# Attention: transpositions issued between similarity matmuls of 384 keys each

## The chip, the cores and the metric

The kernel runs on one core of one Trainium2 chip. The metric is the device time of one execution in microseconds. The kernel before takes 780.84 us, the median of three runs (780.04 to 780.89).

## What is computed

Two batches of eight heads of attention over 768 tokens with 64 dimensions, in which a query sees only the keys of its own cluster (the nearest of 16 centroids), and two feed-forward layers behind it. All is float32.

```python
mask = q_assign[:, :, :, None] == k_assign[:, :, None, :]
scores = scale * np.matmul(q, k.transpose(0, 1, 3, 2))
scores = np.where(mask, scores, -1000000000.0)
scores = scores - np.max(scores, axis=-1, keepdims=True)
attn = np.exp(scores)
attn = attn / (np.sum(attn, axis=-1, keepdims=True) + 1e-09)
return np.matmul(attn, v).astype(np.float32)
```

Behind the attention come h = x @ w_in, a rational function of h, its product with w_out, and a gated layer (w_gate, w_val, w_out of the second layer). The change does not touch these.

## The kernel before

The attention goes through 8 pairs of heads (`pairs`). Of a pair it takes two halves of 384 queries (`half`), of a half three blocks of 128 queries (`i`), of a block the two heads (`e`). This gives 96 steps in the list `order`; n numbers them, and n modulo 12 is the place in the pair. A step n does the following.

- `scores` (L370 to L384): four similarity matmuls on PE. L376 multiplies the high and low parts of 128 queries (`q1`, the weights) by all keys (`k1`), cut by `CUT` into 512 and 256 keys, L380 adds the remaining product and the 16 rows of the mask (`q2`, `k2`, 80 rows), cut in the same way. The result is s_ps, 128 queries by 768 keys, one of two buffers of the pool `ps_s` in PSUM. There are four banks for the two.
- `maximum` (L386): DVE takes the negative maximum of each row of s_ps (L389).
- `transposes` (L425) of step n - 2 (`LAG` = 2): six transpositions of 128 by 128 of the exponentials p on PE (L435), three into one buffer t_ps, three into the next. The buffers come from the pool `ps_t` (L159), which has three; the other users of that pool in the loop are the matmuls of the clusters (`sims`, one buffer per pair) and r_ps in `spread`. Each t_ps is copied to SBUF, by ACT (L440), or the second of a step by DVE (L438) where n modulo 12 is in `dve_evac` = (2, 8, 10, 11).
- `exponentials` (L393): ACT writes p and the sums of the rows (L397).

The main loop (L601) goes over n in twos and calls these in the order scores, maximum, transposes, exponentials; where n modulo 6 is 2 and n is over 6, `spread` (L409) follows, which transposes the reciprocals of the sums (L412, r_ps) and copies them by ACT (L414). After each second step two of the six key blocks of the earlier half are multiplied by v (L446, o_ps, eight matmuls). `background` adds loads, splits and cluster steps for the next pair at fixed n.

Nothing reorders this: every engine takes its instructions in the order in which the code calls them, and waits on semaphores that follow from the tiles and buffers. PE's weight loads are rows of their own in the trace (PEld).

Of the kernel before, what the change touches and what calls it, by code (L numbers as in the profile page):

```python
# [8 lines left out]
F32 = mybir.dt.float32  # L9
F32R = mybir.dt.float32r  # L10
AF = mybir.ActivationFunctionType
ALU = mybir.AluOpType
AX = mybir.AxisListType
# [7 lines left out]
def tile_kernel(ctx, tc, q_t, k_t, q_s, k_s, v_l, cent, w_in, w_out, a_co, b_co, w_gate, w_val, w_o2, out):  # L21
    nc = tc.nc
    B, H, D, S = q_t.shape
    D //= 2
    NC = cent.shape[0] // H
    P = 128
    NB = S // P
    HALF = S // 2
    HB = NB // 2
# [9 lines left out]
    def r32(ap):  # L39
        return ap.bitcast(F32)  # L40
# [100 lines left out]
    def pool(stack, name, bufs, side, space=None):  # L141
        kw = {} if space is None else {"space": space}
        return stack.enter_context(tc.tile_pool(name=name, bufs=bufs, side=side, reuse_waits="tile", **kw))
# [16 lines left out]
    ps_s = pool(Bs, "ps_s", 2, "right", PSUM)  # L160

    heads = {}
    live = {}
    pairs = [(b, hp) for b in range(B) for hp in range(H // 2)]
    order = [(b, hp, half, i, e) for b, hp in pairs for half in range(2) for i in range(HB) for e in range(2)]
    PER = 2 * HB
    KM = D + NC
    CUT = [(0, 512), (512, S)]

    n_x = [0]  # L170

# [37 lines left out]
    def t_tile(name):  # L209
        return ps_t.tile([P, HB, P], F32, tag="t", name=name)  # L210

    def keep_warm(n, to, x=None):
        for _ in range(n):
            for j in range(HB):
                nc.tensor.transpose(to[:, j, :], ident if x is None else x[:, 0:P], ident)  # L215

    warm = ps_s.tile([P, S], F32, tag="s", name="w_ps")[:, 0:HALF].rearrange("p (j c) -> p j c", c=P)
    keep_warm(5, warm)

    wt_i = const.tile([P, NC], mybir.dt.int32, name="wt_i")  # L220
# [11 lines left out]
    for e in range(2):  # L232
# [12 lines left out]
        out=ss[:, 2:3], in0=ss[:, 0:1], scalar=ss[:, 2:3], in1=ss[:, 1:2], op0=ALU.mult, op1=ALU.add  # L245
# [121 lines left out]
                        out=r32(heads[b, 2 * hp + e][key])[D:KM, half * HALF:(half + 1) * HALF], in_=t3[g:g + NC, :]  # L367
                    )

    def scores(b, hp, half, i, e):  # L370
        t = heads[b, 2 * hp + e]
        s_ps = ps_s.tile([P, S], F32, tag="s", name="s_ps")
        q0 = half * HALF + i * P
        qs = slice(q0, q0 + P)
        for lo, hi in CUT:
            nc.tensor.matmul(s_ps[:, lo:hi], t["q1"][:, qs], t["k1"][:, lo:hi], start=True, stop=False)  # L376
        if (b, hp, half, i, e) == order[0]:
            keep_warm(6, fill, oh[0])
        for lo, hi in CUT:
            nc.tensor.matmul(s_ps[:, lo:hi], t["q2"][0:KM, qs], t["k2"][0:KM, lo:hi], start=False, stop=True)  # L380
        if (i, e) == (0, 0):
            st = live["st", b, hp, half] = st_p.tile([P, 3, PER], F32, tag="st", name="st")
            nc.vector.memset(st[:, 2, :], 1e-9)
        live["s", b, hp, half, i, e] = s_ps  # L384

    def maximum(b, hp, half, i, e):  # L386
        st = live["st", b, hp, half]
        k = e * HB + i
        nc.vector.tensor_reduce(  # L389
            out=st[:, 0, k:k + 1], in_=live["s", b, hp, half, i, e], axis=AX.X, op=ALU.max, negate=True  # L390
        )

    def exponentials(b, hp, half, i, e):  # L393
        st = live["st", b, hp, half]
        k = e * HB + i
        p = live["p", b, hp, half, i, e] = p_p.tile([P, S], F32, tag="p", name="p")
        nc.scalar.activation(  # L397
            out=p, in_=live.pop(("s", b, hp, half, i, e)), func=AF.Exp, bias=st[:, 0, k:k + 1],
            accum_out=st[:, 1, k:k + 1],
        )  # L400

    def reciprocals(b, hp, half):
        st = live["st", b, hp, half]
        nc.vector.tensor_reduce(
            out=st[:, 0, :], in_=st[:, 1:3, :].rearrange("p a k -> p k a"), axis=AX.X, op=ALU.add
        )
        nc.vector.reciprocal(out=st[:, 0, :], in_=st[:, 0, :])

    def spread(b, hp, half):  # L409
        st = live.pop(("st", b, hp, half))  # L410
        r_ps = t_tile("r_ps")[0:PER, 0, :]
        nc.tensor.transpose(r_ps, st[:, 0, :], ident)  # L412
        rs = rs_p.tile([PER, P], F32, tag="rs", name="rs")
        nc.scalar.copy(out=rs, in_=r_ps)  # L414
        rd = tc.dram_tile([2, HALF], F32, name="rd")
        nc.sync.dma_start(out=rd.rearrange("e (i p) -> (e i) p", p=P), in_=rs)
        live["rd", b, hp, half] = rd

    def bring_back(b, hp, half):
        rd = live.pop(("rd", b, hp, half))  # L420
        rb = live["rb", b, hp, half] = rb_p.tile([P, HALF], F32, tag="rb", name="rb")
        for e in range(2):
            nc.sync.dma_start(out=rb[e * D:(e + 1) * D, :], in_=rd[e:e + 1, :].to_broadcast([D, HALF]))

    def transposes(b, hp, half, i, e, on_dve):  # L425
        p = live.pop(("p", b, hp, half, i, e))
        if i == 0:
            live["pt", b, hp, half, e] = pt_p.tile([P, NB, HALF], F32, tag="pt", name="pt")
        pt = live["pt", b, hp, half, e]
        qc = slice(i * P, (i + 1) * P)  # L430
        for g in range(2):
            t_ps = t_tile("t_ps")
            for j in range(HB):
                kb = g * HB + j
                nc.tensor.transpose(t_ps[:, j, :], p[:, kb * P:(kb + 1) * P], ident)  # L435
            ks = slice(g * HB, (g + 1) * HB)
            if g == 1 and on_dve:
                nc.vector.tensor_copy(out=pt[:, ks, qc], in_=t_ps)  # L438
            else:
                nc.scalar.copy(out=pt[:, ks, qc], in_=t_ps)  # L440
# [11 lines left out]
    def normalised(b, hp, half):  # L452
        x = live["x", b, hp, half] = x_p.tile([P, HALF], F32, tag="x", name="x")
        nc.vector.tensor_tensor(
            out=x, in0=live.pop(("o", b, hp, half)), in1=live.pop(("rb", b, hp, half)), op=ALU.mult
        )
# [36 lines left out]
    def k_rest(t, x):  # L493
# [6 lines left out]
        out=h0["q1"][up, :], in0=xs[0][0:D, :], scalar=scale, in1=r32(h0["q1"][0:D, :]),  # L500
# [15 lines left out]
    cols = [slice(0, HALF), slice(HALF, S)]  # L516
# [6 lines left out]
    def q_rows(t, half):  # L523
        nc.scalar.activation(
            out=t["q2"][D:D + 32, cols[half]], in_=t["t3"][32 * half:32 * half + 32, :],
            func=AF.Identity, scale=MASKED, bias=msk[32 * half:32 * half + 32, 1:2],
        )
# [9 lines left out]
    dve_evac = (2, 8, 10, 11)  # L537
# [54 lines left out]
    LAG = 2  # L592
    def next_weighted():
        if pv:
            step = pv.pop(0)
            weighted(*step)
            if step[3] == NB - 1:
                return step[:3]


    for n0 in range(0, len(order) + LAG, 2):  # L601
        for n in (n0, n0 + 1):
            if n < len(order):
                scores(*order[n])
                maximum(*order[n])
            if n == 1:
                keep_warm(3, fill)
            if n >= LAG:
                transposes(*order[n - LAG], n % (2 * PER) in dve_evac)
            if n < len(order):  # L610
                exponentials(*order[n])
            if n == 1:
                q_rows(h1, 1)
                for t in (h0, h1):
                    del t["t3"]
            if n % PER == 0 and n:
                reciprocals(*order[n - 1][:3])
            if n % PER == RS and n > PER:
                spread(*order[n - RS - 1][:3])
            elif n == len(order) + 1:  # L620
                spread(*order[-1][:3])
            if n % PER == BB and n > PER:
                bring_back(*order[n - BB - 1][:3])
            for engine in ("dma", "pe", "dve", "pool", "act"):
                background(n, engine)
        finished = next_weighted()
        finished = next_weighted() or finished
        if finished:
            normalised(*finished)
            split_x(*finished)  # L630
        if n >= LAG and (n - LAG) % PER == PER - 1:
            pv.extend([order[n - LAG][:3] + (kb,) for kb in range(NB)])
# [13 lines left out]
    with ExitStack() as mctx:  # L646
# [15 lines left out]
            out=root[:, 1:2], in0=babs[:, 1:2], scalar=root[:, 2:3], in1=root[:, 1:2], op0=ALU.mult, op1=ALU.add  # L662
        )
        nc.vector.tensor_scalar(
            out=root[:, 0:1], in0=root[:, 1:2], scalar1=0.5, scalar2=0.0, op0=ALU.mult, op1=ALU.add
# [273 lines left out]
        for n in range(NS):  # L939
            t, f = seq[n][:2]  # L940
# [19 lines left out]
            if pipe:  # L960
                _, reciprocal, quotient, remainder = pipe.pop()
# [140 lines left out]
        LAG = {"act": 1.7, "dve": 1.7, "pool": 3.5, "dma": 5.5, "set": 0.0}  # L1102
# [105 lines left out]
        _, reciprocal, quotient, remainder = pipe.pop()  # L1208
        mm, _ = project(*seq[NS - 3])
# [12 lines left out]
        mm, _ = project(*seq[NS - 2])  # L1222
# [137 lines left out]
        j, c = 2 * u, 2  # L1360
        r0_ = j * C3 + c * P
        for a in range(2):
            ns = slice(a * 256, (a + 1) * 256)
            bank, to = ps_a.tile([P, T], F32, tag="acc", name="acc")[:, 0:256], part2(j, c)[:, a, :]
            for ff in (f - 1, f):
                g, w = g_hl[j, ff], wt_of["p", ff]
                for m, (wi, gi) in enumerate(((0, 0), (1, 0), (0, 1))):
                    nc.tensor.matmul(  # L1368
                        bank, g[:, gi, c * P:(c + 1) * P], w[:, wi, ns], start=(ff < f and m == 0),
                        stop=(ff == f and m == 2),  # L1370
# [51 lines left out]
```

## Time and profile before

| | |
|---|---|
| median of 3 runs | 780.84 us |
| span of the profiled execution, from its first to its last instruction | 779.4 us |
| PE busy | 773.3 us (99%) |
| weight loads (PEld) busy | 637.7 us (82%) |
| DVE busy | 594.4 us (76%) |
| ACT busy | 510.9 us (66%) |
| POOL busy | 457.4 us (59%) |
| transpositions L435, 576 | 78.7 us |
| similarity matmuls L376, 192 | 58.4 us in the page's group, 512 keys: 490 ns mean, 256 keys: 281 ns |

The granted TensorE clock is 1.00 over the span. Matmuls are pipelined: a row's duration reaches from the start of a matmul to its end, and the next one starts before that, so durations do not add up to the time on the path. What a matmul costs PE is read from the distance of the starts. The attention stage ends with the last transpositions at 227 us.

### The profile page before, as it was taken

Reading aid. Unit: us, or ns where it says so; the run is one execution under the profiler, and the core shown is the slowest. Engines: PE = TensorE matmul, PEld = TensorE weight load, DVE = VectorE, ACT = ScalarE, POOL = GpSimd, SP = SyncE. Lnnn points to the kernel's source line nnn. Section 1 sums busy time; section 2 is a strip of 40 time slices with the busy share of each in tenths; the row PEclk is TensorE's granted clock in tenths of the full one; section 3 lists DMA queues with packets and bytes.
Section 4 is the critical chain, followed back from the end, with each engine's and each line's share of the span. In section 5 each row is a group of like instructions: output and inputs, shape, how many; then the busy total and the mean of one; then the engine's idle time right before and its main releaser. Section 6 shows DMA issues by size and latency. Waiting matters only on the chain.

```text
span 779.4 us, 11585 instructions
## 1 busy us (share of the span) xinstructions
PE 773.3 (99%) x4119; PEld 637.7 (82%) x4119; DVE 594.4 (76%) x894; ACT 510.9 (66%) x984; POOL 457.4 (59%) x429
## 2 busy tenths in 40 slices
PE   8999999999999999999999999999999999999998
PEld 7666666666767888888888888999999999999997
DVE  7778787778659999989999999997565655675454
ACT  8777777777776788787777768646645545454331
POOL 6476797678334676767777688764354544534410
PEclk9999999999999999999999999999999999999999
DMA  7266436533322211211211111013222112120013
GB/s 224 76 203 205 153 99 202 178 115 114 98 79 78 81 56 66 70 55 56 81 55 53 56 33 49 27 55 100 90 82 81 55 55 82 55 81 28 1 41 122
DMA packets 27209, 67.94 MB, mean 87 GB/s; under 512 B 4464, under 2 KB 10832, under 8 KB 27152
## 3 DMA queue, kind: packets, MB, share of 16 engines
q1 hardware_dynamic: 27152, 67.21, 26.3%
q8 instruction: 32, 0.52, 0.3%
q14 instruction: 25, 0.20, 0.1%
HBM read 59.48 MB, written 3.19 MB: 80 GB/s over the span
## 4 chain that ended last, share of the span: by engine, by line
PE 98%; DVE 1%; SPq 1%; DMA 0%; ACT 0%; issue 0%; POOL 0%; POOLq 0%
PE c_ps L1012 23%; PE h_ps L695 17%; PE acc L751 17%; PE acc L1069 13%; PE o_ps L446 8%; PE t_ps L435 8%; PE s_ps L376 5%; PE s_ps L380 4%; PE w_ps L215 1%; PE sim L305 1%; SPq L366 1%; DMA k<-t 0%; DVE st L389 0%; PE r_ps L412 0%; PE acc L1368 0%
## 5 line engine op out<-in xcount | busy, mean ns | idle before, releaser
L1012 PE MATMUL c_ps<-r,wb 128*128 128x384 f32 x648 | 125.3, 336 | 0.0
L1012 PEld LDWEIGHTS c_ps<-r,wb 128*128 128x128 f32 x648 | 115.4, 188 | 6.0
L389 DVE TENSOR_REDUCE st<-s_ps 128x1 f32<-128x768 f32 x96 | 91.5, 953 | 31.3 <-PE s_ps L380 30.5
L397 ACT ACTIVATE p<-s_ps,st 128x768 f32<-128x768 f32 x96 | 87.7, 913 | 13.6 <-DVE st L389 13.3
L712 POOL TENSOR_TENSOR tmp<-tmp 128x512 f32<-128x512 f32 x46 | 67.9, 1475 | 48.1 <-ACT tmp L711 47.7
L440 ACT COPY pt<-t_ps 128x384 f32<-128x384 f32 x160 | 70.0, 482 | 37.8 <-PE t_ps L435 37.5
L1020 ACT COPY tmp<-c_ps 128x384 f32<-128x384 f32 x60 | 28.8, 480 | 87.3 <-PE c_ps L1012 87.3
L1091 POOL TENSOR_TENSOR part<-tmp,part 128x512 f32<-128x512 f32 x18 | 23.3, 1297 | 101.0 <-ACT tmp L1090 101.0
L435 PE MATMUL t_ps<-ident,p 128*128 128x128 f32 x576 | 78.7, 272 | 0.0
L446 PE MATMUL o_ps<-pt,v 128*64 128x384 f32 x384 | 72.3, 499 | 0.0
L435 PEld LDWEIGHTS t_ps<-ident,p 128*128 128x128 f32 x576 | 66.8, 141 | 4.7 <-issue 0.6
L735 POOL TENSOR_TENSOR g<-td,tmp 128x512 fp32r<-128x512 f32 x45 | 58.5, 1300 | 18.0 <-DVE td L730 18.0
L751 PE MATMUL acc<-g,r 128*128 128x512 f32 x288 | 69.0, 389 | 0.0
L1023 DVE TENSOR_TENSOR tmp<-tmp,c_ps 128x384 f32<-128x384 f32 x40 | 22.2, 555 | 58.9 <-ACT tmp L1020 45.1
L1012 PE MATMUL c_ps<-r,xw 128*128 128x384 f32 x336 | 65.4, 337 | 0.0
L751 PEld LDWEIGHTS acc<-g,r 128*128 128x128 f32 x288 | 54.0, 188 | 11.2
L1012 PEld LDWEIGHTS c_ps<-r,xw 128*128 128x128 f32 x336 | 60.0, 188 | 3.7
L695 PE MATMUL h_ps<-r 128*128 128x512 f32 x252 | 60.8, 391 | 0.0
L1069 PE MATMUL acc<-wb,g 128*128 128x512 f32 x216 | 59.4, 394 | 0.0
L376 PE MATMUL s_ps<-k,q 128*128 128x512 f32 x192 | 58.4, 385 | 0.2 <-ACT p L397 0.2
L695 PEld LDWEIGHTS h_ps<-r 128*128 128x128 f32 x252 | 47.1, 188 | 11.5 <-issue 1.8
L376 PEld LDWEIGHTS s_ps<-k,q 128*128 128x128 f32 x192 | 28.8, 189 | 31.7 <-ACT pt L440 18.0
(169 smaller groups left out, 1774.3 us busy)
## 6 DMA issues: line engine op xcount, KB each, us to landing
raw<-w_in_dram SPq DMA_DIRECT2D x16, 512.0 KB
raw<-w_out_dram SPq DMA_DIRECT2D x16, 512.0 KB
raw<-w_val_dram SPq DMA_DIRECT2D x12, 512.0 KB
raw<-w_gate_dram SPq DMA_DIRECT2D x12, 512.0 KB
raw<-w_o_dram SPq DMA_DIRECT2D x12, 512.0 KB
xa<-q_t_dram SPq DMA_DIRECT2D x14, 384.0 KB
xa<-k_t_dram SPq DMA_DIRECT2D x14, 384.0 KB
sq<-q_s_dram SPq DMA_DIRECT2D x8, 384.0 KB
```

The lines of the kernel that those rows point to most:

```text
L376: nc.tensor.matmul(s_ps[:, lo:hi], t["q1"][:, qs], t["k1"][:, lo:hi], start=True, stop=False)
L389: nc.vector.tensor_reduce(out=st[:, 0, k:k + 1], in_=live["s", b, hp, half, i, e], axis=AX.X, op=ALU.max, negate=True)
L397: nc.scalar.activation(out=p, in_=live.pop(("s", b, hp, half, i, e)), func=AF.Exp, bias=st[:, 0, k:k + 1], accum_out=st[:, 1, k:k + 1],)
L435: nc.tensor.transpose(t_ps[:, j, :], p[:, kb * P:(kb + 1) * P], ident)
L440: nc.scalar.copy(out=pt[:, ks, qc], in_=t_ps)
L446: nc.tensor.matmul(live["o", b, hp, half][e * D:(e + 1) * D, :], heads[b, 2 * hp + e]["v"][:, kb, :], live["pt", b, hp, half, e][:, kb, :] ...
L695: nc.tensor.matmul(h_ps, w[:, wi, cs], x[:, xi, cc, :], start=(n == 0), stop=(n == 3 * NCC - 1))
L712: spread.tensor_tensor(out=tq, in0=tq, in1=tr, op=ALU.add)
L735: eng.tensor_tensor(out=g[:, 1, :], in0=td, in1=tr, op=ALU.mult)
L751: nc.tensor.matmul(acc[c], w[:, wi, cs], g[:, gi, :], start=(first and m == 0), stop=(last and m == 2))
L1012: nc.tensor.matmul(live2[key], set_of[f][:, wi, a, cs], x[xi][:, kc, :], start=(first and n == 0), stop=(n == last), skip_group_check=True,)
L1069: nc.tensor.matmul(acc2[j, c], g[:, gi, c * P:(c + 1) * P], w[:, wi, :], start=(f % 2 == 0 and m == 0), stop=(f % 2 == 1 and m == 2),)
```

## The change

Each similarity matmul now takes 384 keys: the first two go to the first and the second bank of s_ps, which is now two banks of 512 with 384 columns used in each, the last two add to them. `transposes` has become a generator that stops after every transposition but the last. The loop makes it before `scores`, and `scores` takes one transposition from it behind each similarity matmul; what is left, two transpositions and the second copy, comes after `maximum`. The maximum and the exponentials read s_ps as two pieces of 384. The keys' halves `cols` were there before (0 to 384, 384 to 768).

```diff
-    def scores(b, hp, half, i, e):
+    def scores(b, hp, half, i, e, behind):
         t = heads[b, 2 * hp + e]
-        s_ps = ps_s.tile([P, S], F32, tag="s", name="s_ps")
+        s_ps = ps_s.tile([P, 2, 512], F32, tag="s", name="s_ps")[:, :, 0:HALF]
         q0 = half * HALF + i * P
         qs = slice(q0, q0 + P)
-        for lo, hi in CUT:
-            nc.tensor.matmul(s_ps[:, lo:hi], t["q1"][:, qs], t["k1"][:, lo:hi], start=True, stop=False)
+        for n in range(2):
+            nc.tensor.matmul(s_ps[:, n], t["q1"][:, qs], t["k1"][:, cols[n]], start=True, stop=False)
+            behind()
         if (b, hp, half, i, e) == order[0]:
             keep_warm(6, fill, oh[0])
-        for lo, hi in CUT:
-            nc.tensor.matmul(s_ps[:, lo:hi], t["q2"][0:KM, qs], t["k2"][0:KM, lo:hi], start=False, stop=True)
+        for n in range(2):
+            nc.tensor.matmul(
+                s_ps[:, n], t["q2"][0:KM, qs], t["k2"][0:KM, cols[n]], start=False, stop=True
+            )
+            behind()
...
-            out=st[:, 0, k:k + 1], in_=live["s", b, hp, half, i, e], axis=AX.X, op=ALU.max, negate=True
+            out=st[:, 0, k:k + 1], in_=live["s", b, hp, half, i, e], axis=AX.XY, op=ALU.max, negate=True
...
                 nc.tensor.transpose(t_ps[:, j, :], p[:, kb * P:(kb + 1) * P], ident)
+                if (g, j) != (1, HB - 1):
+                    yield
...
         for n in (n0, n0 + 1):
+            turns = transposes(*order[n - LAG], n % (2 * PER) in dve_evac) if n >= LAG else iter(())
             if n < len(order):
-                scores(*order[n])
+                scores(*order[n], lambda: next(turns, None))
                 maximum(*order[n])
             if n == 1:
                 keep_warm(3, fill)
-            if n >= LAG:
-                transposes(*order[n - LAG], n % (2 * PER) in dve_evac)
+            for _ in turns:
+                pass
```

On PE, before: the transposition of r_ps at the end of step n = 8, and step n = 9 up to the first matmuls with v (o_ps). The number behind a name tells buffers and tiles apart; in brackets stands the engine whose semaphore is waited for.

```order
L412 MATMUL r_ps_499<-ident_130,st_298 6x128 [waits DVE_49,Activation_49]
L376 MATMUL s_ps_509<-k1_189,q1_187 128x512 [waits Activation_49]
L376 MATMUL s_ps_509<-k1_189,q1_187 128x256
L380 MATMUL s_ps_509<-k2_190,q2_188 128x512
L380 MATMUL s_ps_509<-k2_190,q2_188 128x256
L435 MATMUL t_ps_516<-ident_130,p_474 128x128 [waits Activation_49]
L435 MATMUL t_ps_516<-ident_130,p_474 128x128 x2
L435 MATMUL t_ps_521<-ident_130,p_474 128x128 [waits DVE_49]
L435 MATMUL t_ps_521<-ident_130,p_474 128x128 x2
```

The same place on PE in the changed kernel:

```order
L415 MATMUL r_ps_499<-ident_130,st_298 6x128 [waits DVE_49,Activation_49]
L375 MATMUL s_ps_509<-k1_189,q1_187 128x384 [waits Activation_49]
L438 MATMUL t_ps_512<-ident_130,p_474 128x128 [waits Activation_49]
L375 MATMUL s_ps_509<-k1_189,q1_187 128x384
L438 MATMUL t_ps_512<-ident_130,p_474 128x128
L380 MATMUL s_ps_509<-k2_190,q2_188 128x384
L438 MATMUL t_ps_512<-ident_130,p_474 128x128
L380 MATMUL s_ps_509<-k2_190,q2_188 128x384
L438 MATMUL t_ps_520<-ident_130,p_474 128x128 [waits DVE_49]
L438 MATMUL t_ps_520<-ident_130,p_474 128x128 x2
```

Four of the six transpositions have moved between and behind the similarity matmuls; the last similarity matmul now has three transpositions ahead of it. The wait for ACT ahead of the first transposition and the wait for DVE ahead of the fourth were there before.

On DVE, before, around the same place: the maximum of n = 8 (s_ps_480), the copy of that step's second transpositions, and on to the maximum of n = 9 (s_ps_509).

```order
L389 TENSOR_REDUCE st_439<-s_ps_480 128x1 [waits PE_49]
L438 COPY pt_486<-t_ps_492 128x3x128 [waits PE_49]
L348 TENSOR_TENSOR sm_429<-wt_153,mx_402 128x384 [waits DVE_49]
L354 TENSOR_SCALAR sm_429<-sm_429,msk_156 128x384 [waits DVE_49]
L389 TENSOR_REDUCE st_439<-s_ps_509 128x1 [waits PE_49]
```

On DVE in the changed kernel:

```order
L392 TENSOR_REDUCE st_446<-s_ps_480 128x1 [waits PE_49]
L443 COPY pt_482<-t_ps_491 128x3x128 [waits PE_49]
L347 TENSOR_TENSOR sm_429<-wt_153,mx_402 128x384 [waits DVE_49]
L353 TENSOR_SCALAR sm_429<-sm_429,msk_156 128x384 [waits DVE_49]
L392 TENSOR_REDUCE st_446<-s_ps_509 128x1 [waits PE_49]
```

Nothing has moved on DVE: the copy still stands behind the maximum of its step.

## Rows read from the trace of the kernel before

**Rows 1.** The page: busy time, share, instructions; chain that ended last, by engine.

```profile
PE 773.3 (99%) x4119; PEld 637.7 (82%) x4119; DVE 594.4 (76%) x894; ACT 510.9 (66%) x984; POOL 457.4 (59%) x429
...
PE 98%; DVE 1%; SPq 1%; DMA 0%; ACT 0%; issue 0%; POOL 0%; POOLq 0%
```

**Rows 2.** Waits of PE: tile, line <- what ended it: us in total, times, longest.

```profile
PE w_ps L215 <- POOL ident masks.py:199: 1.4, 1, 1.4
PE s_ps L380 <- DMA k<-t: 0.7, 1, 0.7
...
PE s_ps L376 <- ACT p L397: 0.2, 1, 0.2
```

**Rows 3.** Timeline of PEld, step n = 88: start, us from first to last, instruction, count.

```profile
208.20 0.30 PEld L376 LDWEIGHTS s_ps<-k,q 128*128 128x128 f32 x2 [0.60 <-ACT pt L440]
208.54 0.31 PEld L380 LDWEIGHTS s_ps<-k,q 80*128 80x128 f32 x2
208.89 0.70 PEld L435 LDWEIGHTS t_ps<-ident,p 128*128 128x128 f32 x6
209.56 0.30 PEld L376 LDWEIGHTS s_ps<-k,q 128*128 128x128 f32 x2
```

**Rows 4.** Timeline of PE at 600 us: matmuls of 384 and of 512 columns.

```profile
600.27 1.03 PE L1012 MATMUL c_ps<-r,xw 128*128 128x384 f32 x5
601.14 0.86 PE L1069 MATMUL acc<-xw,g 128*128 128x512 f32 x3
601.84 0.85 PE L1069 MATMUL acc<-tdw,g 128*128 128x512 f32 x3
```

**Rows 5.** Groups of PE by line and shape: count | busy us, mean ns | idle before.

```profile
L1012 PE MATMUL c_ps<-r,wb 128*128 128x384 f32 x648 | 125.3, 336 | 0.0
...
L380 PE MATMUL s_ps<-k,q 80*128 80x256 f32 x96 | 27.1, 282 | 0.0
...
L412 PE MATMUL r_ps<-ident,st 128*6 128x128 f32 x16 | 4.4, 273 | 0.0
```

**Rows 6.** Timeline, steps n = 86 and 87; in brackets idle time before, and what ended it.

```profile
204.73 0.96 DVE L389 TENSOR_REDUCE st<-s_ps 128x1 f32<-128x768 f32 x1 [0.34 <-PE s_ps L380]
...
205.19 0.30 PEld L376 LDWEIGHTS s_ps<-k,q 128*128 128x128 f32 x2
...
205.61 0.55 DVE L438 COPY pt<-t_ps 128x384 f32<-128x384 f32 x1
...
206.23 0.14 PEld L435 LDWEIGHTS t_ps<-ident,p 128*128 128x128 f32 x1
```

**Rows 7.** Timeline: accumulator of n = 27, first load of n = 29.

```profile
73.21 0.19 ACT L397 ACTIVATION_READ_ACCUMULATOR p<-s_ps,st 128x1 f32 x1
...
73.73 0.30 PEld L376 LDWEIGHTS s_ps<-k,q 128*128 128x128 f32 x2
```

**Rows 8.** Timeline: maximum and exponentials of n = 6, first load of n = 8.

```profile
23.04 0.94 DVE L389 TENSOR_REDUCE st<-s_ps 128x1 f32<-128x768 f32 x1
...
24.15 0.97 ACT L397 ACTIVATE p<-s_ps,st 128x768 f32<-128x768 f32 x1
...
24.95 0.26 ACT L397 ACTIVATION_READ_ACCUMULATOR p<-s_ps,st 128x1 f32 x1
...
25.26 0.30 PEld L376 LDWEIGHTS s_ps<-k,q 128*128 128x128 f32 x2 [0.26 <-ACT p L397]
```

**Rows 9.** Timeline: accumulator of n = 95, first load of its transpositions.

```profile
226.18 0.19 ACT L397 ACTIVATION_READ_ACCUMULATOR p<-s_ps,st 128x1 f32 x1
...
226.43 0.14 PEld L435 LDWEIGHTS t_ps<-ident,p 128*128 128x128 f32 x1
```

**Rows 10.** The page's costliest groups: two copies by ACT, three-dimensional and flat.

```profile
L440 ACT COPY pt<-t_ps 128x384 f32<-128x384 f32 x160 | 70.0, 482 | 37.8 <-PE t_ps L435 37.5
L1020 ACT COPY tmp<-c_ps 128x384 f32<-128x384 f32 x60 | 28.8, 480 | 87.3 <-PE c_ps L1012 87.3
```

More of the change, by code (lines that the diff above doesn't have):

```diff
@@ L167, in tile_kernel @@
     KM = D + NC
-    CUT = [(0, 512), (512, S)]
     n_x = [0]
@@ L215, in keep_warm @@
                 nc.tensor.transpose(to[:, j, :], ident if x is None else x[:, 0:P], ident)
-    warm = ps_s.tile([P, S], F32, tag="s", name="w_ps")[:, 0:HALF].rearrange("p (j c) -> p j c", c=P)
+    warm = ps_s.tile([P, 2, 512], F32, tag="s", name="w_ps")[:, 0, 0:HALF].rearrange("p (j c) -> p j c", c=P)
     keep_warm(5, warm)
@@ L397, in exponentials @@
         nc.scalar.activation(
-            out=p, in_=live.pop(("s", b, hp, half, i, e)), func=AF.Exp, bias=st[:, 0, k:k + 1],
-            accum_out=st[:, 1, k:k + 1],
+            out=p.rearrange("p (a n) -> p a n", a=2), in_=live.pop(("s", b, hp, half, i, e)), func=AF.Exp,
+            bias=st[:, 0, k:k + 1], accum_out=st[:, 1, k:k + 1],
         )
```

## The prediction

> **What bounds the kernel now.** I read the page's first and fourth parts, then the list of waits, then the timeline of the stretch that the change touches. PE is busy for 773.3 of 779.4 us and is 98% of the chain that ended last [rows 1]. The list of PE's waits has five lines; the longest is 1.4 us, at the start, the next 0.7 us, the shortest 0.2 us [rows 2]. So nothing late on another engine costs time today, and whatever lengthens PE's own queue moves the end one for one. The attention stage fills PE from about 9.5 to 225.7 us with 96 steps; I call them by n, 0 to 95. 94 of them (n = 2 to 95) hold four similarity matmuls and the six transpositions of step n-2.
>
> **What a step costs on PE.** The weight loads give its rhythm, since one starts when the matmul before it starts. In the step at 208.20 the first load of the similarities' first pair starts at 208.20, that of the second pair at 208.54, that of the first transposition at 208.89, that of the next step at 209.56 [rows 3]: 0.34 + 0.35 + 0.67 = 1.36 us. The six transpositions take 0.67 us, 0.11 each: each has 128 columns and waits for its own load, which starts only with the transposition before. After the last one the next similarity's load also takes 0.11, so 0.34 - 0.11 = 0.23 us are left for the matmul of 512 keys, and 0.35 - 0.23 = 0.12 for that of 256. The loads of both lie under columns.
>
> **The change, part by part.**
>
> *Slots on PE.* Loads and matmuls stay as many; their order becomes similarity, transposition, four times, and two more transpositions. Under 384 columns the transposition's load is hidden; but the load of the similarity behind it now starts with the transposition, and shows its 0.11 us as it does today behind the sixth. Uncovered loads: today five of transpositions and one of a similarity, afterwards two and four. So the six slots of 0.11 us stay, and what differs is 2 x (0.23 + 0.12) = 0.70 us against four matmuls of 384. Rows of that width stand late in the kernel: five in 601.14 - 600.27 = 0.87 us, 0.174 each; three of 512 there take 601.84 - 601.14 = 0.70, 0.233 each [rows 4], about the 0.23 here. The lower bound is 4 x 0.173 = 0.69 us (-0.01 a step), the upper 4 x 0.184 = 0.736 (+0.035), if a change of operand at every slot costs 0.01. I take 0.178, 0.712 us: +0.012 x 94 = **+1.1 us**, bounds -0.9 and +3.3. So I expect nothing from the interleaving itself.
>
> *The maximum comes later.* VectorE's maximum needs the last similarity matmul, now in the seventh slot. It started 0.11 + 0.23 + 0.12 + 0.23 = 0.69 us into the step; now 0.11 + 3 x (0.178 + 0.11) = 0.97. A matmul of 384 columns also takes 336 ns from start to end against 282 for 256 [rows 5]. Together **0.34 us later**. VectorE was idle before the maximum of 204.73, which PE released [rows 6], so it shifts in full.
>
> *Who waits for that: the fourth transposition of fifteen steps.* The transpositions' results go round three buffers (ps_t, L159); a step takes two, one for each three keys' blocks. When `spread` (L409) adds r_ps as a third, the second half of the next step gets the buffer of the second half of the step before, whose copy in those steps runs on VectorE, behind the maximum: the order shows the wait on DVE. Today, in n = 86: maximum at 204.73, copy 205.61 to 206.16, load of the fourth transposition at 206.23 [rows 6], 0.07 us to spare. Afterwards the copy ends at 206.16 + 0.34 = 206.50. The next step's first load starts at about 205.20 (205.19 today [rows 6]), its last similarity 0.97 later at 206.17, and the fourth transposition's load could start then and its matmul at 206.17 + 0.178 = 206.35. The load waits: 206.50 + 0.05 for the release (25.21 to 25.26 [rows 8]) = 206.55, its matmul 206.66: **0.31 us of idle PE**, nothing hides it, and the two transpositions and o_ps queue behind. Were only the matmul held, it would be 206.55 - 206.35 = 0.20; 0.40 if the copy slips another 0.09 (VectorE has other work). r_ps comes 16 times [rows 5], the last behind the last similarity: 15 x 0.30 = **+4.5 us**, bounds 3.0 and 6.0. Below zero it cannot go while the shift exceeds 0.07.
>
> *Who else waits.* A step's first similarity needs the exponentials of two steps before. The tightest place in the steady state is n = 27, whose accumulator is read until 73.21 + 0.19 = 73.40 with the load at 73.73 [rows 7]: 0.33 against a shift of 0.34. Since n = 27 is itself one of the fifteen, its successors come 0.30 later, and I cost it at **nothing**; without that cover it is 0.01 to 0.1 us at a few odd steps. At the start no o_ps fills PE, and n = 8 waits for the exponentials today: maximum 23.04 to 23.98, exponentials from 24.15, (of n = 6) read until 25.21, load at 25.26 [rows 8]. Shifted, the maximum ends at 24.32 and the exponentials start at about 24.42, +0.27. Two such rounds in a row: **+0.5 us** (0.2 to 0.7). At the end the exponentials of n = 95 end at 226.37 and the load of their transposition follows at 226.43 [rows 9]: **+0.3 us**. In n = 13 PE waits 0.71 us for a DMA in front of the third similarity [rows 2]; now two transpositions stand before it: **-0.2 us**. Copies, exponentials and maxima read three-dimensional patterns; that is 482 ns against 480 for a flat copy of the same size [rows 10], so nothing. ScalarE's, GpSimd's and SyncE's queues keep their order.
>
> **Sum.** 1.1 + 4.5 + 0.5 + 0.3 - 0.2 = +6.2 us. The profiled execution's span is 779.4 us; the median of the runs, 780.84, has 1.4 more around it, which stay. 780.84 + 6.2 = **787.0 us**.
>
> **The rivals.**
>
> *Loads vanish on both sides (faster).* If a similarity's load were taken up before the transposition ahead of it starts, both would be covered, and the four slots in front of similarities would shrink to their columns. From the two widths, (0.23 - 0.12) / 256 x 128 = 0.055, plus 0.01 that is left of 0.12 at 256 columns: 0.065 instead of 0.11. 4 x 0.045 x 94 = -17 us: 787.0 - 17 = 770. It decides from the point at which a second load may wait behind a running matmul. Against it: the loads' rows start one matmul apart throughout; six transpositions in a row never fall below 0.11 [rows 3]. Chance 0.08. The Trainium skill bears on this (TensorE: Matmul & The Clock Gate, Step-by-step: what each phase is for): PE's queue pulls weight loads ahead of running matmuls, into a background buffer. By that rule alone the change ought to win, but here the trace shows one load ahead and not two. The same page (Back-to-back issue gap) has 81 ns for a sustained pair with 128 columns; by that the gain would be an estimated 4 x 0.029 x 94 = 11 us; the trace's 0.11 us disagrees.
>
> *The wait has no teeth.* If the copy still ends before the fourth load (the maximum shifts less, or the scheduler's release is another), the sum is 1.1 + 0.5 + 0.3 - 0.2 = 1.7: 782.5, with the slots' bounds 780.5 to 784.7. For it: only 0.3 us decides, and 0.07 are spare. Against: every term of the shift has a row. Chance 0.18, of which 0.08 lands within 0.2%.
>
> *Maximum, exponentials and the next similarity become the bound (slower still).* If the banks apart make the two reads slower by 0.1 us each, the shift is 0.54, the fifteen waits grow by 0.2 (+3), and the first similarities at two odd steps of each of the eight pairs of heads, with 0.33 to 0.48 to spare, wait about 0.07 (+1): 791. For it: the shift alone uses up the spare time of [rows 7]; against, [rows 10]. Chance 0.14.
>
> **How the numbers follow.** The forecast, 784.7 to 789.5, has 0.58, the rivals 0.08, 0.18 and 0.14, and 0.02 are left for no change by other ways. The range of 781.5 to 791.5 takes in all of the forecast, most of the second rival and the third, and leaves out the first. A measurement of this kernel can tell about 0.2%, 1.6 us, from no change: faster 0.08, same 0.10, slower 0.82.
>
> **What would show it.** In the profile after: the load row of the next step 1.36 to 1.40 us behind in steps without o_ps; similarity and transposition in pairs of 0.29 us; fifteen idle gaps of some 0.3 us on PE before the fourth transposition of odd steps, released by the copy on DVE; maxima starting 1.35 us into a step and not 1.01; the attention stage ending some 6 us later and everything behind it unchanged. Pairs of 0.25 us or less would prove the slots wrong; no gaps, the wait.

## The result, and the profile after

The changed kernel takes **786.3 us** (median of 4 runs, 786.22 to 786.87) against 780.5 of the kernel before beside it (780.04 to 780.89): a ratio of **1.0074 [1.0059, 1.0088]**, 0.7% slower. The profiled spans are 785.1 and 779.4 us. The prediction was 787.0, in a range of 781.5 to 791.5, with 0.82 on slower.

The page of the changed kernel, busy time by engine and the chain that ended last, answers to [rows 1].

```profile
PE 778.5 (99%) x4119; PEld 641.2 (82%) x4119; DVE 592.6 (75%) x894; ACT 516.5 (66%) x984; POOL 457.7 (58%) x429
...
PE 97%; DVE 1%; POOL 1%; ACT 1%; issue 0%; POOLq 0%; ACTq 0%
```

PE still bounds the kernel, with as many instructions. Its busy time has grown by 5.2 us, and part of that is no work: the row of a similarity is 0.42 us long, while the next matmul starts 0.26 us behind it where nothing holds it (227.16 and 227.42 us), and so the row covers part of a wait that follows. That is why the largest new row stands among the waits of the weight loads and not among those of PE. Waits of the weight loads (tile and line, what ended the wait, us in total, times, longest), kernel after:

```profile
PEld t_ps L438 <- DVE pt L443: 4.0, 14, 0.3
...
PEld s_ps L375 <- ACT p L400: 1.9, 4, 0.7
```

The first of the two rows is new; the second was 1.1 us in four waits before. In the waits of PE, the same columns, ScalarE's exponentials now hold up a similarity three times and not once as in [rows 2]:

```profile
PE s_ps L375 <- ACT p L400: 0.9, 3, 0.4
```

To see where the 5.7 us lie I cut both traces at the same places: the first similarity matmul of n = 0, 14 and 94, and the o_ps that follow the last transpositions (more o_ps come later, between the matmuls of the next layer). PE timeline (start, us from first to last, instruction, count) of before:

```profile
9.53 0.60 PE L376 MATMUL s_ps<-k,q 128*128 128x512 f32 x2
...
40.54 0.62 PE L376 MATMUL s_ps<-k,q 128*128 128x512 f32 x2
...
221.39 0.62 PE L376 MATMUL s_ps<-k,q 128*128 128x512 f32 x2
...
227.46 1.51 PE L446 MATMUL o_ps<-pt,v 128*64 128x384 f32 x8
```

and of after (the window of this view ends within the last row's group):

```profile
9.88 0.60 PE L375 MATMUL s_ps<-k,q 128*128 128x384 f32 x2
...
41.33 0.45 PE L375 MATMUL s_ps<-k,q 128*128 128x384 f32 x1
...
226.85 0.44 PE L375 MATMUL s_ps<-k,q 128*128 128x384 f32 x1
...
233.18 1.19 PE L451 MATMUL o_ps<-pt,v 128*64 128x384 f32 x6
```

| stretch | before | after | difference |
|---|---|---|---|
| up to n = 0 | 9.53 | 9.88 | +0.35 |
| n = 0 to 14 | 31.01 | 31.45 | +0.44 |
| n = 14 to 94 | 180.85 | 185.52 | +4.67 |
| n = 94 to those o_ps | 6.07 | 6.33 | +0.26 |
| behind, to the end of the span | 551.9 | 551.9 | 0 |

The first line is no effect of the change, which has done nothing by then: over all profiles of this study n = 0 starts between 9.1 and 10.1 us. The second line hides more than it shows, since before holds a wait for a DMA in it that after does not have (below). Everything behind the attention stage is as long as it was.

### The profile page after: what moved, and what is told of

The parts are those of the page before. It is cut to its first block, busy times and chain, and to the rows that moved or that the text cites. A ratio compares the mean times of both kernels' runs of the same rounds, so it can differ in the third digit from the quotient of the medians.

```text
span 785.1 us, 11637 instructions
## 1 busy us (share of the span) xinstructions
PE 778.5 (99%) x4119; PEld 641.2 (82%) x4119; DVE 592.6 (75%) x894; ACT 516.5 (66%) x984; POOL 457.7 (58%) x429
## 4 chain that ended last, share of the span: by engine, by line
PE 97%; DVE 1%; POOL 1%; ACT 1%; issue 0%; POOLq 0%; ACTq 0%
PE c_ps L1018 23%; PE h_ps L701 17%; PE acc L757 17%; PE acc L1075 13%; PE o_ps L451 9%; PE t_ps L438 8%; PE s_ps L375 5%; PE s_ps L380 4%; PE sim L304 1%; DVE st L392 1%; PE w_ps L214 1%; ACT p L400 1%; POOL k L499 0%; POOL q L502 0%; PE r_ps L415 0%
## 5 line engine op out<-in xcount | busy, mean ns | idle before, releaser
L438 PE MATMUL t_ps<-ident,p 128*128 128x128 f32 x576 | 125.6, 274 | 0.7
L445 ACT COPY pt<-t_ps 128x384 f32<-128x384 f32 x160 | 72.4, 477 | 20.9 <-PE t_ps L438 19.2
L438 PEld LDWEIGHTS t_ps<-ident,p 128*128 128x128 f32 x576 | 76.4, 140 | 7.2 <-DVE pt L443 4.0
L375 PE MATMUL s_ps<-k,q 128*128 128x384 f32 x192 | 69.5, 428 | 0.9 <-ACT p L400 0.9
L380 PE MATMUL s_ps<-k,q 80*128 80x384 f32 x192 | 68.4, 423 | 0.4 <-POOL k L499 0.4
L375 PEld LDWEIGHTS s_ps<-k,q 128*128 128x128 f32 x192 | 36.1, 188 | 33.5 <-ACT pt L445 18.0
```

The lines of the kernel that those rows point to most:

```text
L375: nc.tensor.matmul(s_ps[:, n], t["q1"][:, qs], t["k1"][:, cols[n]], start=True, stop=False)
L380: nc.tensor.matmul(s_ps[:, n], t["q2"][0:KM, qs], t["k2"][0:KM, cols[n]], start=False, stop=True)
```

## The experiments

Unless said otherwise each diff is against the changed kernel, and the kernel before took 780.5 to 780.7 us beside it. "Steps" means n = 14 to 94, "start" n = 0 to 14, both as in the table.

**The cut alone.** The similarities keep 384 keys and their banks, but all transpositions follow behind them, as before.

```diff
-                scores(*order[n], lambda: next(turns, None))
+                scores(*order[n], lambda: None)
```

> The cut of 384 keys and the two-bank tile stay, the six transpositions stand behind the maximum again. Theory (the order of the transpositions costs the time, through the later maximum): four slots of 0.174 to 0.178 us stand where 0.70 us stood, the maximum starts where it did (1.01 us into a step), no wait for the copy: 780 to 782 us, kernel before 780.5. Rival (the cut, the banks or the three-dimensional reads cost it): 783 to 786.

Measured 780.89 us, 1.0002 [0.9993, 1.0012]. The cut and the banks apart cost nothing that can be told; steps took 181.68 us, of which 0.59 are one wait that this profile alone has, at n = 91, so some 3 ns a step over before. The loss is the interleaving.

**The interleaving alone.** Four transpositions between the similarities, which are cut at 512 and 256 in one tile again.

```diff
+    CUT = [slice(0, 512), slice(512, S)]
...
-        s_ps = ps_s.tile([P, 2, 512], F32, tag="s", name="s_ps")[:, :, 0:HALF]
+        s_ps = ps_s.tile([P, S], F32, tag="s", name="s_ps")
...
-            nc.tensor.matmul(s_ps[:, n], t["q1"][:, qs], t["k1"][:, cols[n]], start=True, stop=False)
+            nc.tensor.matmul(s_ps[:, CUT[n]], t["q1"][:, qs], t["k1"][:, CUT[n]], start=True, stop=False)
```

> The transpositions stay between the similarity matmuls, but these take 512 and 256 keys as in the kernel before. Theory: the last similarity matmul still has three transpositions ahead of it, the maximum starts some 0.3 us later, fifteen waits of about 0.2 us before the fourth transposition: 784 to 787 us. Rival (equal cuts are what makes the order slow or fast): 780 to 782.

Measured 786.86 us, 1.0078 [1.0063, 1.0093], the whole loss of the change. The waits of its weight loads have the same row (its lines are one further on), and the steps that hold them are longer by 0.26 us, as in the changed kernel:

```profile
PEld t_ps L439 <- DVE pt L444: 3.3, 14, 0.4
```

Together the two runs put the loss on the order of the instructions and not on their widths.

**Other copies on VectorE.** The table `dve_evac` says at which n modulo 12 the second copy is VectorE's. The fourth transposition of n = 87 waits for the copy in step n = 86, which is entry 2; with 3 and 9 in place of 2 and 8 that copy goes to ScalarE.

```diff
-    dve_evac = (2, 8, 10, 11)
+    dve_evac = (3, 9, 10, 11)
```

> The changed kernel with the list of copies on DVE (3, 9, 10, 11) in place of (2, 8, 10, 11): as many copies on DVE, but in the steps with r_ps the second copy is ACT's and does not stand behind the maximum. Theory (ring of three buffers, copy behind the late maximum): the fourteen waits of 0.25 us that its trace shows vanish, 786.3 - 3.4 = 782.9 us, 782.3 to 783.6. Rival (the waits are only where time shows that PE loses in its slots anyway): 785.5 to 786.5.

Measured 783.34 us, 1.0037 [1.0023, 1.0052], 3.0 below the changed kernel. The row with DVE is gone from the waits, the three other rows of these loads stayed; steps took 182.02 us, 3.50 less. So the fourteen waits are worth 3.0 to 3.5 us.

**The third user of the buffers one step later.** RS is the place of `spread` behind its last step; r_ps then no longer stands between the two steps.

```diff
-    XS, RS, BB = 3, 2, 4
+    XS, RS, BB = 3, 3, 4
```

> The changed kernel with r_ps transposed one step later (n modulo 6 is 3 and not 2); copies stay where they are. Theory: r_ps now takes the third buffer behind an odd step, the buffer that the next step's second half gets is that of an ACT copy, and o_ps gives it time: no waits, 782.9 us, 782.3 to 783.6. Rival (DVE's copy is late for whatever follows): 785.5 to 786.5.

Measured 784.03 us, 1.0045 [1.003, 1.006], 0.4 above the upper end of what was expected: a miss. The mechanism held: no wait of these loads for the copy on VectorE, and steps of 182.27 us. The start took 32.34, since PE waited in n = 13 for rows of k. Timelines of this kernel, SyncE's queue and PE:

```profile
35.76 2.27 SPq L365 DMA_DIRECT2D k<-t  x2
...
38.81 0.41 PE L380 MATMUL s_ps<-k,q 80*128 80x384 f32 x1 [0.36 <-DMA k<-t]
```

Two DMA issues that otherwise take 1.22 us together took 2.27. With this wait of some 0.9 us taken off, the profiled execution (783.85 us) is where it was expected. The three other executions have no trace and took 783.68 to 784.89, so the miss of the median is explained only if they had such a wait too; that is open.

**Interleaved only from n = 10 on.** This parts the start from the rest.

```diff
-                scores(*order[n], lambda: next(turns, None))
+                scores(*order[n], (lambda: next(turns, None)) if n >= 10 else (lambda: None))
```

> The changed kernel, but steps 0 to 9 keep the transpositions behind the maximum. In the changed kernel step 12 starts 1.4 us later, counted from step 2, than in the kernel before, and step 13 then no longer waits 0.9 us for its DMA. Theory (at the start the round of maximum, exponentials and next similarity bounds, and the later maximum lengthens it): the 1.4 us are not lost, some 0.6 of the DMA's wait come back: 785.3 to 785.9 us. Rival (it is lost to PE's slots): 786.2 to 786.5, with the same start of step 12.

Measured 785.29 us, 1.006 [1.0046, 1.0074], 1.0 below the changed kernel and at the lower edge of what was expected. The wait for the DMA in n = 13, of which the expectation had 0.6 us coming back, is not among PE's waits here. The start took 30.24 us against 31.45, the steps 185.59. So the start costs 1.0 to 1.2 us, and not the 0.5 of the prediction.

**One transposition between instead of four,** behind the first similarity.

```diff
-            behind()
+            if n == 0:
+                behind()
...
-            behind()
```

> The changed kernel with one transposition between similarity matmuls (behind the first) and five behind the maximum. Theory (the time lost follows how much later the maximum starts): the maximum starts about 0.11 us later than in the kernel before, not 0.34, the fourth transposition's load is called later too, waits of at most 0.1 us: 781 to 783 us. Rival (changing between similarity and transposition costs by the change): a fourth of the whole loss, 782, with all steps longer by the same and no waits.

Measured 784.32 us, 1.0049 [1.0034, 1.0065]: a miss. The maximum came 0.12 us later, as reckoned, and the waits for VectorE were gone; but as many came up in another place. Waits of the weight loads of this kernel:

```profile
PEld t_ps L438 <- ACT pt L445: 3.1, 15, 0.2
```

The timeline of this kernel in n = 86 and 87 (in brackets the idle time before, and what ended it) shows which:

```profile
207.05 0.96 DVE L392 TENSOR_REDUCE st<-s_ps 128x1 f32<-128x768 f32 x1 [0.45 <-PE s_ps L381]
207.27 0.48 ACT L445 COPY pt<-t_ps 128x384 f32<-128x384 f32 x1 [0.35 <-PE t_ps L438]
207.29 0.09 PEld L415 LDWEIGHTS r_ps<-ident,st 128*6 128x6 f32 x1
207.40 0.19 PEld L375 LDWEIGHTS s_ps<-k,q 128*128 128x128 f32 x1
207.80 0.14 PEld L438 LDWEIGHTS t_ps<-ident,p 128*128 128x128 f32 x1 [0.21 <-ACT pt L445]
```

r_ps moves the whole round of three buffers on by one, so the first half of n = 87 also gets the buffer of the first half of n = 86. With four between, that half is full early and its copy is early too; with one between, the half is full only near the end of its step, its copy runs from 207.27 to 207.75, and the first transposition of n = 87, which is now second in its step, stands 0.2 us for it. I had looked at the second half of the round only. Fourteen of the fifteen stand in n = 14 to 94. Of the 3.2 us that these steps took more than before, 14 x 0.18 = 2.5 are the waits, and the rest is 0.7, some 8 ns a step.

**The DMA wait filled.** This one is against the kernel before: only in n = 13 all six transpositions stand ahead of the third similarity, where the trace of before has PE wait 0.71 us for k<-t [rows 2].

```diff
-                scores(*order[n])
+                early_t = n == 13
+                scores(*order[n], (lambda: transposes(*order[n - LAG], False)) if early_t else None)
...
-            if n >= LAG:
+            if n >= LAG and n != 13:
```

> The kernel before, only in step 13, which waits 0.71 us for the DMA of the mask's rows, the six transpositions are issued ahead of the third similarity matmul. Theory: their 0.66 us run while PE waits: 0.6 us less than the kernel before, 779.9. Rival (another wait ends just behind): no change.

Measured 780.58 us, 0.9999 [0.9991, 1.0008]: a miss. The interval alone reaches 0.7 us down and so would still hold the 0.6; the medians are 0.03 apart. The reason lies in the wait. Timeline of SyncE's queue, kernel before:

```profile
33.85 1.22 SPq L366 DMA_DIRECT2D k<-t  x2
35.12 2.04 SPq L423 DMA_DIRECT2D rb<-rd  x2
```

Such a pair takes 1.22 or 1.23 in the other places around. In each of the eleven profiles one issue of this queue between 35.7 and 40.3 us takes 1.1 to 1.7 us, where the others there take 0.42 to 0.60, at a place of its own: in this run at 39.23, after the rows of k, and there was nothing to fill.

```profile
39.23 1.29 SPq L181 DMA_DIRECT2D xa<-k_t_dram  x1
```

The semaphore updates in the traces tell when the rows of k landed. In the kernel before, the last of their DMAs has fifteen of its sixteen updates by 36.38 us and the sixteenth at 37.80, and PE goes on at 37.93; in this run all sixteen are there by 36.69, ahead of the step (36.87).

By the list of its waits PE stood for k's rows at n = 13 in two traces, before, where the long issue follows right behind them, and the fourth experiment, where it is one of them and they are issued until 38.03. (In the third it is one of them too, but they are all issued by 37.06, before the step begins. The last experiment has a shorter wait of another origin.) If other executions are like these, a median holds little of such a wait. That makes 30.1 us (31.01 less the 0.93 by which the third similarity of n = 13 was late in all) the start of before to compare with; the cut alone had 30.20.

**Both losses mended:** the other copies on VectorE, and interleaving from n = 10 on, in one kernel (the two diffs above).

> The changed kernel with both: copies on DVE at (3, 9, 10, 11) and no transposition between in steps 0 to 9. Theory: losses add, 786.3 - 3.4 - 0.7 = 782.2 us, what is left over the kernel before being the slots (84 steps of 0.015 us) and the last step: 781.5 to 783. Rival (the interleaving itself gains once its waits are gone): below 780.5.

Measured 782.07 us, 1.0019 [1.001, 1.0028]. The start took 30.30 us and the steps 181.99. The losses add, and what is left is the slots (1.14 us over 80 steps), the end and 0.2 at the start.

**One between, and the third user later:** the diff of one transposition between, and RS = 3.

> e6_one_between with r_ps transposed one step later, as in e4_spread_later. The trace of e6_one_between shows fifteen waits of 0.2 us before the first transposition of the step behind r_ps, for ACT's copy of the buffer that r_ps pushed the ring on to. Theory (the ring of three with r_ps in it): the waits go, 784.3 - 3 = 781.3 us, 780.9 to 782.2. Rival (ACT's copies are late as such, the ring only shows where): 783.8 to 784.5.

Measured 782.25 us, 1.0022 [1.0012, 1.0031], just above the upper edge of what was expected and not the 781.3 in its middle. The waits for copies went, as reckoned. The start took 30.93 us, with waits of the loads of 0.22 us at n = 12 and 0.25 at n = 13: each ends 0.1 us behind the last landing of rows of k (35.16 and 37.69 us). These rows go out later, since rd<-rs, which writes out the reciprocals from r_ps, stands ahead of them in SyncE's queue and has moved with it. SyncE's queue with one transposition between alone:

```profile
28.83 0.35 SPq L419 DMA_DIRECT2D rd<-rs  x1
30.40 1.22 SPq L365 DMA_DIRECT2D q<-t  x2
```

and here:

```profile
30.98 0.35 SPq L419 DMA_DIRECT2D rd<-rs  x1
31.38 1.22 SPq L365 DMA_DIRECT2D q<-t  x2
```

Neither expectation for the move of r_ps, this one and that of the fourth experiment, had counted this. The steps took 181.81, of which 0.53 are one place, in n = 86 and 87 (timelines of PEld and ACT):

```profile
203.25 0.68 ACT L82 ACTIVATE raw<-raw 128x512 f32<-128x512 f32 x1 [0.77 <-DMA raw<-w_in_dram]
...
205.61 0.19 PEld L375 LDWEIGHTS s_ps<-k,q 128*128 128x128 f32 x1 [0.53 <-ACT p L400]
```

Here ScalarE stood 0.77 us for a piece of a weight, with two copies and the exponentials of n = 85 queued behind; the cut alone has such a place at n = 91. Whether other executions have it is open. Without it 0.43 us are left over 80 steps, 5 ns each. No version beat the kernel before.

## Why the prediction was right, step by step

**Slots: right.** Forecast: the 0.11 us of a load that is hidden under a similarity shows up again behind the transposition, so +0.012 us a step. PEld timeline of n = 88 in the kernel after, which answers to [rows 3]:

```profile
213.31 0.19 PEld L375 LDWEIGHTS s_ps<-k,q 128*128 128x128 f32 x1 [0.60 <-ACT pt L445]
213.44 0.14 PEld L438 LDWEIGHTS t_ps<-ident,p 128*128 128x128 f32 x1
213.60 0.19 PEld L375 LDWEIGHTS s_ps<-k,q 128*128 128x128 f32 x1
213.73 0.14 PEld L438 LDWEIGHTS t_ps<-ident,p 128*128 128x128 f32 x1
213.89 0.19 PEld L380 LDWEIGHTS s_ps<-k,q 80*128 80x128 f32 x1
214.02 0.14 PEld L438 LDWEIGHTS t_ps<-ident,p 128*128 128x128 f32 x1
214.17 0.19 PEld L380 LDWEIGHTS s_ps<-k,q 80*128 80x128 f32 x1
214.31 0.41 PEld L438 LDWEIGHTS t_ps<-ident,p 128*128 128x128 f32 x3
214.68 0.19 PEld L375 LDWEIGHTS s_ps<-k,q 128*128 128x128 f32 x1
```

From one similarity's load to the next it is 0.29, 0.29, 0.28 us, the sum of 0.178 and 0.11 that was forecast, where the first rival needed 0.25 or less. The rows here give the sum and not its two parts; where like follows like they are seen: with one transposition between, the last two similarities of n = 86 start 0.18 us apart (206.50 and 206.68), and transpositions in a row 0.11 [rows 3]. The step is 214.68 - 213.31 = 1.37 us long against 1.36. Over the steps without waits the mean is some 15 ns more than before, 1.2 us over 80 of them. The runs part it: the cut alone 3 ns, one transposition between 5 to 8, four 14 to 17, so an estimated 3 for each place in which a similarity and a transposition alternate. The Trainium skill (TensorE: Matmul & The Clock Gate, Step-by-step: what each phase is for) has loads pulled ahead of running matmuls; no row here shows a second load taken up behind a running matmul, and the pairs of 0.29 us speak against it.

**The maximum 0.34 us later: right.** Timeline of n = 86 and 87 after, the answer to [rows 6]:

```profile
208.57 0.19 PEld L375 LDWEIGHTS s_ps<-k,q 128*128 128x128 f32 x1 [0.60 <-ACT pt L445]
209.92 0.96 DVE L392 TENSOR_REDUCE st<-s_ps 128x1 f32<-128x768 f32 x1 [0.67 <-PE s_ps L380]
210.05 0.19 PEld L375 LDWEIGHTS s_ps<-k,q 128*128 128x128 f32 x1
210.79 0.55 DVE L443 COPY pt<-t_ps 128x384 f32<-128x384 f32 x1
210.92 0.19 PEld L380 LDWEIGHTS s_ps<-k,q 80*128 80x128 f32 x1
211.40 0.31 PEld L438 LDWEIGHTS t_ps<-ident,p 128*128 128x128 f32 x3 [0.29 <-DVE pt L443]
```

It starts 209.92 - 208.57 = 1.35 us into its step, the number forecast, and VectorE was idle before it. The rows divide it otherwise than the working did: in n = 94 PE's row of the last similarity starts 0.88 us into the step (227.73 against 226.85), not 0.97, and lasts 0.42 us, not 0.34. The two differences cancel.

**Fifteen waits of 0.30 us: right in kind, mis-sized.** They are there, before the fourth transposition, released by the copy on DVE: the load comes 0.06 behind the copy's end (211.34 to 211.40). There are fourteen, since n = 9 waits for other things at the start, and each lengthens its step by 0.245 us (3.24 against 2.99), 3.4 us and not 4.5. The load is held by more than the 0.3 that was priced: without the wait it would follow the last similarity's by 0.14, as at 214.31, so at 211.06; it is 0.34 late. But what queues behind gets 0.10 back: the three loads take 0.31 from first to last, 0.41 where a similarity still runs its columns ahead of them. The working had the load 0.38 late (206.55 against 206.17) and only 0.07 of it made up (0.31 at the matmul). That the kernel of the third experiment, in which nothing but the place of these copies differs, gets 3.0 us back shows the cause.

**The start: this step failed in size.** Forecast +0.5 (0.2 to 0.7), measured +1.0 to 1.2 by the fifth experiment. The profile has 1.35 (31.45 against the 30.1 of before). Put beside the cut alone, the distance from the step before grows at five steps: n = 4 by 0.33 us, n = 6 by 0.29, n = 8 by 0.15, n = 9 by 0.25, n = 10 by 0.16.

Three of them are the rounds forecast, in which a first similarity waits for exponentials that start after the later maximum. PE timeline after, n = 6, 8 and 9:

```profile
22.93 0.44 PE L375 MATMUL s_ps<-k,q 128*128 128x384 f32 x1 [0.43 <-ACT p L400]
...
26.37 0.45 PE L375 MATMUL s_ps<-k,q 128*128 128x384 f32 x1 [0.15 <-ACT p L400]
...
28.41 0.44 PE L375 MATMUL s_ps<-k,q 128*128 128x384 f32 x1 [0.29 <-ACT p L400]
```

The steps grow by 0.69 at these three, the upper end of that term; I had started from n = 8 and left out n = 6, though the wait of 0.2 us for ScalarE in [rows 2] is that of n = 6. The other two, 0.49 us, I had not seen at all: the first transposition now stands ahead of three similarities, so whatever it waits for holds them up too. PEld timeline after, n = 3 and n = 9, which delay n = 4 and n = 10:

```profile
17.34 0.14 PEld L438 LDWEIGHTS t_ps<-ident,p 128*128 128x128 f32 x1 [0.34 <-ACT q L529]
...
28.77 0.14 PEld L438 LDWEIGHTS t_ps<-ident,p 128*128 128x128 f32 x1 [0.18 <-ACT pt L445]
```

Before, this load came behind all four similarities of its step, and by then what it needs was done. The order shown ahead of the prediction had this move in it, with the wait for ACT at the transposition; I did not price it.

**The end: right.** Forecast +0.3, measured +0.26. PEld timeline after, the load of the transpositions of n = 95, against [rows 9], where it did not wait:

```profile
232.22 0.68 PEld L438 LDWEIGHTS t_ps<-ident,p 128*128 128x128 f32 x6 [0.35 <-ACT p L400]
```

**The DMA in n = 13: wrong as a term.** The 0.71 us came from one late landing in the one profile. Neither the cut alone, which reaches n = 13 at the same time, nor the seventh experiment has the wait, so a gain of 0.2 was not to be counted on; how often other executions have it is not shown.

**Exponentials in the steady state at nothing: right.** PE's three waits for them after are those of n = 6, 8 and 9; the cover (the fifteen waits themselves) was not needed where it was taken away, in the third and eighth experiments, whose steps lost only what the slots cost.

**The sum.** 1.2 for the slots of the 80 steps counted, 3.4 for the waits, 1.0 to 1.2 for the start and 0.3 for the end make 5.9 to 6.1, where the median moved by 5.8. The forecast of 6.2 was so close partly by luck, because two errors cancelled: the waits 1.1 too large, the start 0.5 to 0.7 too small. Of the 0.7 us between 787.0 and 786.3, 0.3 is the time that the sum started from, 780.84, where the kernel before took 780.5 beside the changed one. That the second rival, a wait without teeth, falls is shown by the fourteen rows; the time of the third (791) would have needed slower reads from the banks apart, and the first experiment has none.

## What to carry to other kernels

Before two kinds of matmul are alternated, price each slot as the longer of the columns of one and the load of the next, each read from rows: a load hidden on one side may show up again on the other, and here it did (0.29 us a pair, from 0.178 and 0.11). Then follow how much later the last matmul of the group ends, through the engine that reads it, what is queued behind on that engine, and the round of buffers back to the next matmul, for every user of the round: 0.07 us to spare became 0.25 us lost at fourteen places. And ask of each instruction that is moved, forward or back, what now queues behind its wait.

## What the chip showed that I had not expected

One DMA issue of SyncE's queue in each profile, at 35.7 to 40.3 us, takes 1.1 to 1.7 us where the others there take 0.42 to 0.60, at another place each time, and every profile has one to three more of 1.0 us or longer later in the attention stage, between 53 and 190 us; their cause is open. So a wait seen in one profile need not be part of the median: filling the 0.71 us moved it by 0.03 us. And a wait that drains PE costs less than it holds: 0.34 us at the load were 0.245 us of the step.
